# Where a Relu stands in ScalarE's queue: one edit for the inner layers, one for the first expert and one for the last weights of an attention and two-MoE kernel

## The chip, the cores and the metric

The kernel runs on one core of a Trainium2 chip. The metric is the device time of one execution in microseconds (us). The kernel before was run three times: 2096.52, 2099.13 and 2100.53 us, with a median of 2099.13 us. A separate profiled execution of it took 2101.21 us, and the trace of that execution covers a span of 2099.0 us.

The engines are named as the profile names them: PE is the matrix engine, PEld its weight load, DVE the vector engine, ACT the scalar engine, POOL the third elementwise engine, and SP the engine that issues nearly all DMAs. SPq is SP's DMA queue. The program lists the instructions of each engine in an order of their own, and the trace shows ACT, DVE and SP running theirs in that order.

## The reference

Three stages follow one another. `x` is 2304 tokens by 512 features between them.

```
# 1 attention: 4 x 8 heads, 1152 positions, 64 wide, queries averaged in pairs
attn = softmax(q.reshape(B, H, S//2, 2, D).mean(3) @ k.T / sqrt(D));  x = attn @ v
# 2 first MoE: P comes from exp(x @ w_gate) by 8 rounds of row and column scaling
for e in range(8): out += P[:, e:e+1] * (relu(x @ w1[e]) @ w2[e])     # w1[e] 512x1024, w2[e] 1024x512
# 3 second MoE: 8 experts with 4 slots each
slot_input = softmax_over_tokens(x @ phi).T @ x                       # 32 slots
slot_out[e] = relu(slot_input[e] @ w1[e]) @ w2[e]
out = softmax_over_slots(x @ phi) @ slot_out
```

## The kernel before, in words

**Numbers in two parts.** Matmuls of the first MoE work on fp32 values split in a high part and a low part: a CAST on ACT gives the high part, a subtraction on DVE the low part, and PE multiplies high by high, high by low and low by high. Such a split of a hidden activation is `h_split` (L731 to L735, tiles `ho`, three buffers); of a weight `p_split` or `f_hi` and `f_lo`; of `x` of block `i` `x0_split` (L589).

**Stages.** Attention ends near 505 us of the span. Then come experts 0 to 7 of the first MoE, one after another, over 9 blocks of 256 tokens, which are grouped in 3 units of 3 blocks. Expert 0 (506 to 699 us) has a plain first layer (`plain`, L786) and a second layer in a Strassen-Winograd form with 7 products (`product`, L805). Experts 1 to 6 (700 to 1775 us) have both layers in that form: 6 experts by 3 units are 18 units. Expert 7 (1775 to 2026 us) is plain and shares its time with the gate of the second MoE. The second MoE itself and the stores end the program.

**First layer of experts 1 to 6.** `chunk(e, u, n, f)` (L749) is one form `n` (0 to 6) for one quarter `f` (0 to 3) of the hidden features: 6 matmuls into a PSUM bank, then one elementwise step. For the last two forms, n = 5 and 6, the step has two instructions: DVE adds the bank to what lies in the hidden tile (L783), then ACT takes the Relu in place (L769, called at L784). The bank pool of these forms has two banks, so a chunk's matmuls need the add of two chunks earlier to be done.

**What orders the work.** The program builds a list of items, most of them one chunk, one plain quarter or one product. `at(k, f, late=...)` hangs other work behind item k. A loop (L1333) then calls each item and, behind it, what hangs there, in order of `late`. What an item itself issues therefore always stands ahead of what hangs behind it: in ACT's queue the Relu of chunk k stands ahead of an `h_split` CAST that hangs behind item k.

**Between the first experts.** `x0_split(0)` and `x0_store` prepare and store the split `x` of block 0; the split runs on DVE in the last part of attention. `prep` (L630) forms sums of `x` for the Strassen form of experts 1 to 6: four DVE sums, two CASTs on ACT and two subtractions, hung behind two items of each of blocks 1 to 4 and one of block 5. `fsum` (L507) forms sums of expert 1's weights on DVE, from staged quarters that SP loads (L474, L478) some items earlier; tuples `jobs` (L1284) and `FORMS0` (L1267) say behind which items. `base[b]` is the first item of block b, and a block has 11 items, p for a product of 12 matmuls and f for a plain quarter of 24, in the order "pfppfppfppf".

**Weights of the second MoE.** They are 32 MB, 64 units of 512 KB: 32 of w1, then 32 of w2. `load_m2(tags)` issues their DMAs on SP into tiles of earlier work that have come free, one name for each pool of buffers: `v`, `w` and `h` for weights and hidden tiles, `a`, `o`, `s` for `xa`, `ho` and `stg`. The tiles of `h` have 6 KB in each partition, and a load used 4 KB of them. The calls hang behind items of expert 7; 22 units are issued only when the first layer of the second MoE releases its w1 tiles (L1404). `layer2` (L1423) reads w2 in 8 steps of feature blocks f for each half dh of the output and each group G of four experts; `folded` (L1439) and `output` (L1453 to L1469) follow each half.

Of the kernel before, what the change touches and what calls it, by code (L numbers as in the profile page):

```python
# [405 lines left out]
def tile_attention__moe__softmoe(ctx, tc, q, k, v, w_gate, w1, w2, phi, m2_w1, m2_w2, out):  # L406
# [182 lines left out]
    def x0_split(i, copy=None):  # L589
        if i == 0:  # L590
            X0[i] = [x_tile("xs")[:, :512].rearrange("p (t z n) -> p t z n", t=2, z=2) for _ in range(4)]
            for kk in range(4):
                part = xa[i][:, kk].rearrange("p (t n) -> p t n", t=2)
                (copy or nc.scalar.copy)(X0[i][kk][:, :, 0], part)
                nc.vector.tensor_tensor(
                    out=X0[i][kk][:, :, 1], in0=part, in1=X0[i][kk][:, :, 0].bitcast(F32), op=ALU.subtract
                )
            return
        x = w_tile(("22", "11")[i % 2]).rearrange("p h (k t z n) -> p h k t z n", k=2, t=2, z=2)
        X0[i] = [x[:, kk // 2, kk % 2] for kk in range(4)]  # L600
        Xb[i] = x.rearrange("p h k t z n -> p h (k t z n)")
        for h in range(2):
            part = xa[i][:, 2 * h:2 * h + 2].rearrange("p k (t n) -> p k t n", t=2)
            nc.scalar.copy(x[:, h, :, :, 0], part)
            nc.vector.tensor_tensor(out=x[:, h, :, :, 1], in0=part, in1=x[:, h, :, :, 0].bitcast(F32), op=ALU.subtract)

    def x0_store(i):
        u = i // 3
        d = Xd[i] = dram_p.tile([128, 4, 512], F32, name=f"xd{i}")
        if i == 0:  # L610
            for kk in range(4):
                nc.sync.dma_start(out=d[:, kk], in_=X0[i][kk].rearrange("p t z n -> p (t z n)").bitcast(F32))
# [123 lines left out]

    seed, unit = {}, {}
    free = [2, 1, 3, 0]
# [10 lines left out]
    def chunk(e, u, n, f):  # L749
# [25 lines left out]
        if n == 1:  # L775
            relu(unit["A", 0][:, f], ps)
        elif n in (2, 3):
            nc.scalar.copy(unit["B", n - 2][:, f], ps)  # L778
        elif n == 4:
            relu(unit["A", 1][:, f], ps)  # L780
        else:
            o = unit["B", 6 - n][:, f]
            nc.vector.tensor_tensor(out=o, in0=ps, in1=o, op=ALU.add)  # L783
            relu(o, o)  # L784

# [188 lines left out]
    def tail2_steps(i):  # L974
# [3 lines left out]
        def tr(t):  # L978
            def f():
                if t == 0:  # L980
                    st["xT"] = stg_p.tile([128, 4, 256], F32, tag="stg", name="x2T")
                    if i == 0:
                        for _ in range(2):
                            HT.append(m_p.tile([128, 4, 256], F32, tag="ho", name="HT", bufs=3))
                            nc.gpsimd.memset(HT[-1], 0.0)  # L985
                        miscr = stg_p.tile([128, 1024], F32R, tag="stg", name="miscr")
                        T2["ct"] = [x_tile("ct") for _ in range(3)]
                        T2["c4"] = x_tile("c4", F32)
                        T2["o2"] = miscr[:, 768:1024]
                        misc = stg_p.tile([128, 1024], F32, tag="stg", name="misc")  # L990
# [115 lines left out]
    def slot_input():  # L1106
# [13 lines left out]
    w1t, w2t = {}, {}  # L1120
    queue = [("w1", e, z) for e in range(E) for z in range(2)] + [
        ("w2", dh, u) for dh in range(2) for u in range(8)
    ]

    def load_part(t, kind, a, b, lo, n):
        if kind == "w1":
            src = m2_w1[a][128 * lo:128 * (lo + n)].rearrange("(k p) f -> p k f", p=128)
            nc.sync.dma_start(out=t.rearrange("p (k f) -> p k f", k=n), in_=src)
            for x in range(n):
                w1t[a, lo + x] = t[:, 1024 * x:1024 * x + 1024]  # L1130
        else:
            f, e = 2 * (b % 4), 4 * (b // 4) + lo
            for c in range(2):
                src = m2_w2[e:e + n, 128 * (f + c):128 * (f + c) + 128, 256 * a:256 * a + 256].rearrange("e p d -> p e d")
                dst = t[:, 256 * n * c:256 * n * c + 256 * n]
                nc.sync.dma_start(out=dst.rearrange("p (e d) -> p e d", e=n), in_=src)
                for x in range(n):
                    w2t[a, e + x, f + c] = dst[:, 256 * x:256 * x + 256]

    rest = []  # L1140
    TAGS = {
        **{f"v{j}": (m_p, f"v{j}", 1) for j in range(7)},
        **{f"w{x}": (wp_p if x in EARLY else m_p, f"w{x}", 1) for x in ("11", "12", "S2", "S3", "22", "S1", "S4")},
        **{f"h{j}": (m_p, f"h{j}", 1) for j in range(4)},
        "a": (xa_p, "xa", NBLK), "o": (m_p, "ho", 3), "s": (stg_p, "stg", 4),
    }

    def load_m2(tags):
        for tag in tags.split():
            if not queue and not rest:  # L1150
                return
            pool, name, bufs = TAGS[tag]
            if tag[0] in "haos":
                kind, a, b = rest[0] if rest else queue.pop(0)
                n = 1 if kind == "w1" else 2
                lo = (2 * b if kind == "w1" else 0) + (n if rest else 0)
                rest[:] = [] if rest else [(kind, a, b)]
                t = pool.tile([128, 1536 if tag[0] == "h" else 1024], F32, tag=name, name="m2h", bufs=bufs)[:, :1024]
            else:
                kind, a, b = queue.pop(0)  # L1160
                n, lo = (2, 2 * b) if kind == "w1" else (4, 0)
                t = pool.tile([128, 2048], F32, tag=name, name="m2w", bufs=bufs)
            load_part(t, kind, a, b, lo, n)

# [80 lines left out]
    for n, (e, i, pos) in enumerate(blocks):  # L1245
# [21 lines left out]
    FORMS0 = (  # L1267
# [5 lines left out]
    for e in range(E - 1):  # L1273
        n = e + 1
        r = starts[e, 2] if e else base[8]
        if n < E - 1:
# [6 lines left out]
            else:  # L1283
                jobs = ((base[5] + 6, base[5] + 10, 2), (base[6] + 6, base[6] + 10, 2))  # L1284
            for (s, d, w), raws, names, stage in zip(jobs, (W1Q, Q), (WS, VS), (stage_w, stage_v)):
# [10 lines left out]

    where = [base[1 + n // 2] + (2, 7)[n % 2] for n in range(9)]
    for n, k in enumerate(where):
# [49 lines left out]
    for k in range(last + NBLK):  # L1348
# [18 lines left out]
        if q < 3 and j in (3, 6):  # L1367
            p_split(E - 1, q + 1 + j // 6 * 4, (("12", "S2", "S3"), ("v1", "v2", "v3"))[j // 6][q])
        load_m2({0: "v4", 1: "v5", 2: "v6", 7: "wS4", 9: "v0", 11: "w11", 18: "v1", 20: "w12", 26: "v2",
                 27: "wS2", 29: "a", 30: "a", 31: "a", 32: "a", 33: "a w22", 34: f"wS3 a wS1 h{order7[1]} o",  # L1370
                 35: f"a v3 h{order7[2]}"}.get(k, ""))
# [147 lines left out]
```

## Time and profile before

| what | value |
|---|---|
| three runs, median | 2096.52, 2099.13, 2100.53; 2099.13 us |
| profiled execution: its time, its span | 2101.21 us, 2099.0 us |
| PE busy | 2046.2 us, 97% of the span |
| DVE, ACT, POOL busy | 1426.4, 997.5, 410.4 us |
| chain of work that ended last, by engine | PE 80%, DVE 9%, ACT 4%, DMA 3% |
| DMA | 367.42 MB, mean 175 GB/s |

A row of the timeline gives start, duration, engine, line, operation, output <- inputs, shape and count; in brackets stands the idle time of that engine ahead of the row and what ended it. A row of the waits gives total us, number of waits, and the longest one. The clock column is the granted TensorE clock as a share of its full 2.4 GHz; 0.50 is the lower of its two levels, 1.2 GHz.

### The profile page before, as it was taken

The numbers are of one execution on the slowest core, as the hardware profiler recorded it, in microseconds if no ns is written. First come the engines' busy times: TensorE is split into PE (matmuls) and PEld (weight loads), VectorE is DVE, ScalarE is ACT, GpSimd is POOL, SyncE is SP. The second block draws the span as 40 slices with busy tenths as digits, with TensorE's granted clock in tenths as the row PEclk, the third lists the DMA queues.
The fourth block names the chain that finished last, engine by engine and source line by source line (L and its number), as shares of the span: only waits on it lengthen the run. The fifth ranks groups of instructions, "written<-read, shape, count | busy, mean of one in ns | idle before, by whom it ended". The sixth has DMA issues, their size and how long they took to land.

```text
span 2099.0 us, 38009 instructions
## 1 busy us (share of the span) xinstructions
PE 2046.2 (97%) x14800; PEld 1861.9 (89%) x14800; DVE 1426.4 (68%) x2601; ACT 997.5 (48%) x2110; POOL 410.4 (20%) x304
## 2 busy tenths in 40 slices
PE   7999999999999999999999999999999999999996
PEld 5777777777999999999999999999999999999863
DVE  5878778779676686776677677667767656544551
ACT  4666666666443644554454455445445444211231
POOL 6888888882000000000000000000000000000000
PEclk9999999999999999999999999999999999999997
DMA  7555565443457664456457345544744333577579
GB/s 187 139 134 125 119 148 136 114 114 126 166 182 258 214 223 151 153 186 209 139 183 249 133 161 192 190 165 151 262 141 159 113 111 113 201 267 254 211 244 278
DMA packets 198978, 367.42 MB, mean 175 GB/s; under 512 B 51472, under 2 KB 116304, under 8 KB 195792
## 3 DMA queue, kind: packets, MB, share of 16 engines
q1 hardware_dynamic: 196400, 363.53, 55.1%
q8 instruction: 117, 1.92, 0.4%
q10 hardware_dynamic: 2400, 1.47, 0.3%
q14 instruction: 61, 0.50, 0.1%
HBM read 276.38 MB, written 55.84 MB: 158 GB/s over the span
## 4 chain that ended last, share of the span: by engine, by line
PE 80%; DVE 9%; ACT 4%; DMA 3%; issue 2%; SPq 1%; POOL 0%; ACTq 0%; DVEq 0%; POOLq 0%
PE y L824 24%; PE seed L763 10%; PE g L763 9%; PE o L271 7%; PE se L245 7%; PE S L216 4%; DVE ht L728 2%; DVE hr L783 2%; PE g L859 2%; PE g L860 2%; PE g L858 2%; PE y L881 1%; PE y L882 1%; PE y L883 1%; ACT hr L769 1%
## 5 line engine op out<-in xcount | busy, mean ns | idle before, releaser
L824 PE MATMUL y<-v,ho 128*128 128x256 f32 x5292 | 691.9, 282 | 6.1 <-DVE ho L735 3.4
L824 PEld LDWEIGHTS y<-v,ho 128*128 128x128 f32 x5292 | 673.7, 190 | 11.6 <-issue 4.7
L763 PE MATMUL g<-xs,w 128*128 128x384 f32 x1728 | 337.2, 337 | 10.5 <-DVE hr L783 9.4
L256 POOL TENSOR_TENSOR acc<-acc,e 128x576 f32<-128x576 f32 x218 | 310.7, 1425 | 28.0 <-ACT e L248 14.1
L763 PEld LDWEIGHTS g<-xs,w 128*128 128x128 f32 x1728 | 292.3, 189 | 19.0 <-DVE hr L783 15.5
L217 DVE TENSOR_REDUCE m<-S 128x1 f32<-128x384 f32 x432 | 227.8, 554 | 76.3 <-PE S L216 60.6
L735 DVE TENSOR_TENSOR ho<-hr,ho 128x512 fp32r<-128x512 f32 x252 | 173.4, 688 | 144.4 <-ACT ho L734 143.8
L985 POOL MEMSET HT<- 128x1024 f32 x2 | 1.9, 958 | 1319.3 <-PE y L824 1319.3
L248 ACT ACTIVATE e<-se 128x288 f32<-128x288 f32 x576 | 213.3, 411 | 95.5 <-PE se L245 94.5
L836 DVE SCALAR_TENSOR_TENSOR acc<-y,P,acc 128x256 f32<-128x256 f32 x378 | 181.3, 480 | 106.7 <-PE y L824 105.2
L763 PE MATMUL seed<-xs,w 128*128 128x384 f32 x1296 | 247.6, 335 | 0.0
L763 PEld LDWEIGHTS seed<-xs,w 128*128 128x128 f32 x1296 | 220.2, 189 | 0.0
L735 DVE TENSOR_TENSOR ho<-ht,ho 128x512 fp32r<-128x512 f32 x189 | 129.6, 689 | 78.7 <-ACT ho L734 76.5
L734 ACT CAST ho<-hr 128x512 fp32r<-128x512 f32 x252 | 154.6, 615 | 45.1 <-PE y L824 31.8
L245 PE MATMUL se<-q,kd 128*128 128x288 f32 x576 | 166.6, 298 | 0.8 <-DVE kp L160 0.5
L769 ACT ACTIVATE hr<-hr 128x384 f32<-128x384 f32 x144 | 74.5, 525 | 195.3 <-DVE hr L783 195.3
L245 PE MATMUL se<-qm,kd 128*128 128x288 f32 x576 | 164.7, 295 | 0.0
L271 PE MATMUL o<-e,vr 128*64 128x288 f32 x1152 | 160.9, 414 | 0.0
L216 PE MATMUL S<-kd,q 128*128 128x384 f32 x384 | 143.3, 377 | 1.6 <-DVE m L217 1.4
L734 ACT CAST ho<-ht 128x512 fp32r<-128x512 f32 x189 | 115.7, 617 | 49.0 <-PE y L824 25.6
L778 ACT COPY hr<-seed 128x384 f32<-128x384 f32 x144 | 69.2, 480 | 127.9 <-PE seed L763 127.4
L271 PEld LDWEIGHTS o<-e,vr 128*64 128x64 f32 x1152 | 74.1, 136 | 50.4 <-issue 8.1
(211 smaller groups left out, 3036.3 us busy)
## 6 DMA issues: line engine op xcount, KB each, us to landing
stg<-in_moe_w_dram SPq DMA_DIRECT2D x96, 512.0 KB, 6.1
w<-xd SPq DMA_DIRECT2D x72, 512.0 KB, 4.7
xs<-xd0T SPq DMA_DIRECT2D x48, 384.0 KB, 3.9
xs<-xd1T SPq DMA_DIRECT2D x48, 384.0 KB, 4.9
xs<-xd2T SPq DMA_DIRECT2D x48, 384.0 KB, 3.6
kd<-kp SPq DMA_DIRECT2D x31, 576.0 KB, 5.9
xs<-xd0B SPq DMA_DIRECT2D x36, 384.0 KB, 3.6
xs<-xd1B SPq DMA_DIRECT2D x36, 384.0 KB, 3.9
```

The lines of the kernel that those rows point to most:

```text
L216: nc.tensor.matmul(ps, lhsT=w, rhs=r[:, 384 * n:384 * n + 384], start=True, stop=True)
L217: nc.vector.tensor_reduce(out=M_[ph][:, x, n:n + 1], in_=ps, axis=AX.X, op=ALU.max)
L245: nc.tensor.matmul(ps, lhsT=kd[:, z, 128 * c:128 * c + 128], rhs=y[:, h, g], start=z == 0, stop=z == 1)
L248: nc.scalar.activation(out=e[:, g], in_=ps, func=AF.Exp, scale=1.0 / 16)
L256: nc.gpsimd.tensor_tensor(out=acc_[ph], in0=acc_[ph], in1=e, op=ALU.add)
L271: nc.tensor.matmul(O_[ph][64 * g:64 * g + 64, :288], lhsT=raws["v"][pi][:, h, c, :], rhs=E_[ph, c][:, g], start=c == 0, stop=c == 8,)
L734: nc.scalar.copy(o[:, 0], p)
L735: nc.vector.tensor_tensor(out=o[:, 1], in0=p, in1=o[:, 0].bitcast(F32), op=ALU.subtract)
L763: nc.tensor.matmul(ps, lhsT=w[:, a, kk, 128 * f:128 * f + 128], rhs=x[:, :, b], start=first and kk + z == 0, stop=kk == 1 and z == 2, skip ...
L769: relu = lambda o, b: nc.scalar.activation(out=o, in_=b, func=AF.Relu)
L824: nc.tensor.matmul(ps, lhsT=o[:, x, c], rhs=v[:, w, c], start=first and c + z == 0, stop=c + z == 5, skip_group_check=not first,)
L836: nc.vector.scalar_tensor_tensor(out=y, in0=ps, scalar=p, in1=y, op0=ALU.mult, op1=ALU.add)
```

## The change

It has four parts.

**Relus of the last two forms.** `chunk` no longer issues the Relu of n = 5 and 6 at once, but puts it in a list `behind`. The loop over the items empties that list after all that hangs behind the item. Where nothing hangs there, ACT's order stays as it was; where an `h_split` hangs, its CAST now stands ahead of the Relu.

```diff
             nc.vector.tensor_tensor(out=o, in0=ps, in1=o, op=ALU.add)
-            relu(o, o)
+            behind.append(lambda: relu(o, o))
...
         for _, fs in sorted(after, key=lambda x: x[0]):
             for g in fs:
                 g()
+        while behind:
+            behind.pop(0)()
```

ACT, the last two forms of one unit of expert 2, before (`ho` and `hr` L734 are the splits, `hr` L769 the Relus):

```order
L734 CAST ho<-hr 128x512
L769 ACTIVATE hr<-hr 128x384
L734 CAST ho<-ht 128x512
L769 ACTIVATE hr<-hr 128x384 x2
L734 CAST ho<-ht 128x512
L769 ACTIVATE hr<-hr 128x384
L734 CAST ho<-hr 128x512
L734 CAST ho<-ht 128x512
L769 ACTIVATE hr<-hr 128x384 x2
L734 CAST ho<-hr 128x512
L769 ACTIVATE hr<-hr 128x384
L734 CAST ho<-hr 128x512
```

The same stretch after (lines are 6 higher):

```order
L740 CAST ho<-hr 128x512
L740 CAST ho<-ht 128x512
L775 ACTIVATE hr<-hr 128x384 x2
L740 CAST ho<-ht 128x512
L775 ACTIVATE hr<-hr 128x384
L740 CAST ho<-hr 128x512
L775 ACTIVATE hr<-hr 128x384
L740 CAST ho<-ht 128x512
L775 ACTIVATE hr<-hr 128x384 x2
L740 CAST ho<-hr 128x512 x2
L775 ACTIVATE hr<-hr 128x384
L740 CAST ho<-hr 128x512
```

Five of the eight Relus of a unit have moved behind the CAST that hung behind the same item. PE's order and DVE's order in these experts are as before.

**Block 0 of x.** `x0_split(0)` uses two tiles of the pool `stg` with two CASTs and two subtractions of 128x512, where it used four tiles of the pool `x` with four and four of 128x256; `x0_store` issues two DMAs in place of four.

**Expert 0's sums.** The nine `prep` sums and the sums of expert 1's weights hang behind other items, as do the loads of the latter.

```diff
-            jobs = ((base[5] + 6, base[5] + 10, 2), (base[6] + 6, base[6] + 10, 2))
+            jobs = ((base[5] + 6, base[6] + 2, 2), (base[6] + 10, base[7] + 3, 2))
-    where = [base[1 + n // 2] + (2, 7)[n % 2] for n in range(9)]
+    where = [base[b] + d for b, d in ((1, 4), (1, 8), (2, 4), (2, 8), (3, 2), (3, 5), (3, 9), (4, 2), (4, 9))]
```

In each tuple of `jobs` the first number is the item behind which the loads are issued, the second that of the first of four sums, the third the distance between them. In `FORMS0` form "11" goes from (-3, 2, 3) to (0, 6, 7) and "12" from (0, 8, 9) to (2, 8, 9).

DVE, around the first sum of weights in expert 0 (`stg` L507; `ho` are splits, `ht` sums of hidden tiles), before:

```order
L735 TENSOR_TENSOR ho<-hr,ho 128x512
L728 TENSOR_TENSOR ht<-hr 128x512
L728 TENSOR_TENSOR ht<-ht,hr 128x512
L507 TENSOR_TENSOR stg<-stg 128x1024
L735 TENSOR_TENSOR ho<-ht,ho 128x512 x2
L728 TENSOR_TENSOR hr<-hr 128x4x128
L728 TENSOR_TENSOR ht<-hr,ht 128x512
L507 TENSOR_TENSOR stg<-stg 128x1024
L836 SCALAR_TENSOR_TENSOR acc_8242<-y,acc_8242 128x256
L735 TENSOR_TENSOR ho<-hr,ho 128x512
```

After:

```order
L741 TENSOR_TENSOR ho<-hr,ho 128x512
L734 TENSOR_TENSOR ht<-hr 128x512
L734 TENSOR_TENSOR ht<-ht,hr 128x512
L741 TENSOR_TENSOR ho<-ht,ho 128x512 x2
L734 TENSOR_TENSOR hr<-hr 128x4x128
L734 TENSOR_TENSOR ht<-hr,ht 128x512
L842 SCALAR_TENSOR_TENSOR acc_8233<-y,acc_8233 128x256
L741 TENSOR_TENSOR ho<-hr,ho 128x512
L507 TENSOR_TENSOR stg<-stg 128x1024
```

The first weight sum has moved down past three splits, and where one stands in this stretch now, two stood before.

**Weights of the second MoE.** w2 is cut into pieces of 1 KB in each partition (one feature block of one expert and half), and `load_m2` fills each tile with as many pieces as it holds: 8, 6, 4, or 3 for a tile of the pool `x` (new tag). Two small tiles (`c4` and `o2`) move from the pools `x` and `stg` to `ht`, which frees two tiles `x` and one `stg`; a load into an `stg` tile is new behind item 28 of expert 7 (k = 28). The strings of tags change with it.

```diff
-                 27: "wS2", 29: "a", ..., 33: "a w22", 34: f"wS3 a wS1 h{order7[1]} o",
+                 27: "wS2", 28: "s", 29: "a", ..., 33: "a w22", 34: f"wS3 wS1 a h{order7[1]} h{order7[0]} o x x",
...
-    load_m2(f"a a h{order7[3]} h{order7[0]}")
+    load_m2(f"a a h{order7[3]}")
...
-                if kk % 2 and (e < 5 or 2 * e + kk // 2 == 13):
-                    load_m2("v4 v5 v6 wS4 v0 w11 v1 w12 v2 wS2 x x x w22".split()[2 * e + kk // 2])
+                if kk % 2 and 2 * e + kk // 2 < 10:
+                    load_m2("v4 v5 v6 wS4 v0 w11 v1 w12 v2 wS2".split()[2 * e + kk // 2])
```

SP's DMAs from the last load of `x` on (L1128 w1, L1136 w2), before:

```order
L676 DMA w<-xd_6544 128x1024 x2
L1128 DMA m2h<-in_moe_w_dram 128x1024 x2
L1128 DMA m2w<-in_moe_w_dram 128x2x1024 x2
L1128 DMA m2h<-in_moe_w_dram 128x1024
L1128 DMA m2w<-in_moe_w_dram 128x2x1024
L1136 DMA m2h<-in_moe_w_dram 128x2x256 x6
L1136 DMA m2w<-in_moe_w_dram 128x4x256 x2
L1136 DMA m2h<-in_moe_w_dram 128x2x256 x10
L1136 DMA m2w<-in_moe_w_dram 128x4x256 x22
```

After (L1148 w1, L1159 w2):

```order
L682 DMA w<-xd_6538 128x1024 x2
L1148 DMA m2h<-in_moe_w_dram 128x1024 x2
L1148 DMA m2w<-in_moe_w_dram 128x2x1024 x3
L1159 DMA m2h<-in_moe_w_dram 128x4x256 x2
L1159 DMA m2h<-in_moe_w_dram 128x2x256 x2
L1159 DMA m2h<-in_moe_w_dram 128x4x256 x2
L1159 DMA m2h<-in_moe_w_dram 128x3x256
L1159 DMA m2h<-in_moe_w_dram 128x256
L1159 DMA m2h<-in_moe_w_dram 128x2x256 x3
L1159 DMA m2w<-in_moe_w_dram 128x2x256
L1159 DMA m2w<-in_moe_w_dram 128x4x256
L1159 DMA m2w<-in_moe_w_dram 128x2x256
```

The bytes are the same. Of 64 units 46.5 now stand ahead of the first layer of the second MoE, where 42 did; the w2 DMAs are of 128 to 512 KB, where they were of 256 and 512 KB, and there are more of them.

## Rows read from the trace of the kernel before

**Rows 1.** Page, section 1: busy us (share of the span) and instructions of each engine.

```profile
PE 2046.2 (97%) x14800; PEld 1861.9 (89%) x14800; DVE 1426.4 (68%) x2601; ACT 997.5 (48%) x2110; POOL 410.4 (20%) x304
```

**Rows 2.** Table by stretch: PE, PEld, DVE, ACT, POOL busy; clock, DMA share, GB/s.

```profile
506.00:700.00 194.00, 187.91 (x1571) 181.72 (x1564) 136.30 (x282) 88.18 (x170) 0.00 (x0) 1.00 0.53 193
700.00:1775.00 1075.00, 1063.59 (x7472) 1054.69 (x7471) 747.54 (x1236) 526.04 (x963) 0.00 (x0) 1.00 0.52 172
2020.00:2044.00 24.00, 20.04 (x197) 10.95 (x199) 10.91 (x40) 7.35 (x29) 0.00 (x0) 0.93 0.96 310
2044.00:2070.00 26.00, 25.93 (x394) 15.19 (x390) 6.40 (x21) 7.58 (x23) 0.00 (x0) 1.00 1.09 349
2078.00:2099.00 21.00, 5.91 (x28) 4.42 (x20) 3.61 (x6) 3.68 (x7) 0.00 (x0) 0.50 0.69 172
```

**Rows 3.** Waits of the span: us in total, times, longest.

```profile
ACT ho L734 <- PE y L824: 57.4, 73, 1.5
...
PE g L763 <- DVE hr L783: 9.4, 19, 0.5
...
PE f L1430 <- DMA m2w<-in_moe_w_dram: 3.7, 5, 0.9
```

**Rows 4.** Timeline of one unit of expert 2, forms 5 and 6.

```profile
982.43 0.55 DVE L783 TENSOR_TENSOR hr<-g,hr 128x384 f32<-128x384 f32 x1
983.01 0.52 ACT L769 ACTIVATE hr<-hr 128x384 f32<-128x384 f32 x1 [1.54 <-DVE hr L783]
983.45 0.60 ACT L734 CAST ho<-ht 128x512 fp32r<-128x512 f32 x1
...
983.57 1.21 PE L763 MATMUL g<-xs,w 128*128 128x384 f32 x6
984.08 0.69 DVE L735 TENSOR_TENSOR ho<-ht,ho 128x512 fp32r<-128x512 f32 x1 [1.10 <-ACT ho L734]
984.69 0.55 DVE L783 TENSOR_TENSOR hr<-g,hr 128x384 f32<-128x384 f32 x1
...
985.30 1.33 PE L763 MATMUL g<-xs,w 128*128 128x384 f32 x6 [0.51 <-DVE hr L783]
```

**Rows 5.** Timeline of the end of attention: split of block 0.

```profile
482.15 1.50 DVE L594 CAST xs<-x 128x256 fp32r<-128x256 f32 x1
...
488.00 0.43 DVE L595 TENSOR_TENSOR xs<-x,xs 128x256 fp32r<-128x256 f32 x1
...
493.61 0.71 PE L282 MATMUL t<-acc,ones 128*64 128x288 f32 x4 [0.84 <-DVE acc L262]
```

**Rows 6.** Timeline of expert 0: the three longest waits of PE and what precedes them.

```profile
605.77 16.24 SPq L651 DMA_DIRECT2D xd2T<-xt  x5
...
617.00 0.62 ACT L648 CAST xt<-xs 128x512 fp32r<-128x512 f32 x1 [4.06 <-DVE xs L643]
...
618.98 1.70 PE L824 MATMUL y<-v,ho 128*128 128x256 f32 x12 [0.98 <-ACT acc L832]
...
628.28 2.01 SPq L474 DMA_DIRECT2D stg<-in_moe_w_dram  x4
...
635.78 1.22 DVE L507 TENSOR_TENSOR stg<-stg 128x1024 f32<-128x1024 f32 x1 [2.91 <-DMA stg<-in_moe_w_dram]
...
637.67 1.46 PE L824 MATMUL y<-v,ho 128*128 128x256 f32 x10 [1.92 <-DVE ho L735]
...
660.79 1.45 PE L824 MATMUL y<-v,ho 128*128 128x256 f32 x10 [0.94 <-DVE ho L735]
```

**Rows 7.** Timeline of the second MoE: its last loads and its end.

```profile
2038.03 32.21 SPq L1136 DMA_DIRECT2D m2w<-in_moe_w_dram  x22
...
2064.36 0.70 PE L1439 MATMUL fd<-misc,wg 128*128 128x256 f32 x2
...
2076.02 0.64 PE L1430 MATMUL f<-m2w,HT 128*32 128x256 f32 x8 [0.78 <-DMA m2w<-in_moe_w_dram]
2077.43 1.08 PE L1430 MATMUL f<-m2w,HT 128*32 128x256 f32 x8 [0.78 <-DMA m2w<-in_moe_w_dram]
...
2079.06 1.22 PE L1439 MATMUL fd<-misc,wg 128*128 128x256 f32 x2 [0.55 <-ACT misc L1435]
```

More of the change, by code (lines that the diff above doesn't have):

```diff
@@ L590, in x0_split @@
         if i == 0:
[L591 to L594, printed above, removed]
+            X0[i], Xb[i] = [], []
+            for h in range(2):
+                t = stg_p.tile([128, 1024], F32R, tag="stg", name="xt")
+                Xb[i].append(t)
+                x = t.rearrange("p (k t z n) -> p k t z n", k=2, t=2, z=2)
+                X0[i] += [x[:, 0], x[:, 1]]
+                part = xa[i][:, 2 * h:2 * h + 2].rearrange("p k (t n) -> p k t n", t=2)
+                (copy or nc.scalar.copy)(x[:, :, :, 0], part)
                 nc.vector.tensor_tensor(
-                    out=X0[i][kk][:, :, 1], in0=part, in1=X0[i][kk][:, :, 0].bitcast(F32), op=ALU.subtract
+                    out=x[:, :, :, 1], in0=part, in1=x[:, :, :, 0].bitcast(F32), op=ALU.subtract
                 )
@@ L610, in x0_store @@
         if i == 0:
-            for kk in range(4):
-                nc.sync.dma_start(out=d[:, kk], in_=X0[i][kk].rearrange("p t z n -> p (t z n)").bitcast(F32))
+            for h in range(2):
+                nc.sync.dma_start(
+                    out=d[:, 2 * h:2 * h + 2].rearrange("p k n -> p (k n)"), in_=Xb[i][h].bitcast(F32)
+                )
         else:
@@ L735, in h_split @@
         nc.vector.tensor_tensor(out=o[:, 1], in0=p, in1=o[:, 0].bitcast(F32), op=ALU.subtract)
-    seed, unit = {}, {}
+    seed, unit, behind = {}, {}, []
     free = [2, 1, 3, 0]
@@ L985, in f @@
                             nc.gpsimd.memset(HT[-1], 0.0)
-                        miscr = stg_p.tile([128, 1024], F32R, tag="stg", name="miscr")
                         T2["ct"] = [x_tile("ct") for _ in range(3)]
-                        T2["c4"] = x_tile("c4", F32)
-                        T2["o2"] = miscr[:, 768:1024]
+                        T2["c4"] = m_p.tile([128, 512], F32, tag="ht", name="c4", bufs=2)
+                        T2["o2"] = m_p.tile([128, 512], F32R, tag="ht", name="o2", bufs=2)[:, :256]
                         misc = stg_p.tile([128, 1024], F32, tag="stg", name="misc")
@@ L1120, in tile_attention__moe__softmoe @@
     w1t, w2t = {}, {}
[L1121 to L1138, printed above, removed]
+    queue = [("w1", e, 2 * z) for e in range(E) for z in range(2)]
+    pieces = [(dh, G, f, g) for dh in range(2) for G in range(2) for f in range(8) for g in range(4)]
     rest = []
     TAGS = {
[L1142 to L1145, printed above, removed]
+        **{f"v{j}": (m_p, f"v{j}", 1, 8) for j in range(7)},
+        **{f"w{x}": (wp_p if x in EARLY else m_p, f"w{x}", 1, 8) for x in ("11", "12", "S2", "S3", "22", "S1", "S4")},
+        **{f"h{j}": (m_p, f"h{j}", 1, 6) for j in range(4)},
+        "a": (xa_p, "xa", NBLK, 4), "o": (m_p, "ho", 3, 4), "s": (stg_p, "stg", 4, 4), "x": (wp_p, "x", 5, 3),
     }
@@ L1149, in load_m2 @@
         for tag in tags.split():
-            if not queue and not rest:
+            if not queue and not rest and not pieces:
                 return
[L1152 to L1163, printed above, removed]
+            pool, name, bufs, size = TAGS[tag]
+            t = pool.tile([128, 256 * size], F32, tag=name, name="m2w" if size == 8 else "m2h", bufs=bufs)
+            if queue or rest:
+                n = size // 4
+                e, k = rest.pop() if rest else queue.pop(0)[1:]
+                if n == 1 and k % 2 == 0:
+                    rest.append((e, k + 1))
+                src = m2_w1[e][128 * k:128 * (k + n)].rearrange("(k p) f -> p k f", p=128)
+                nc.sync.dma_start(out=t.rearrange("p (k f) -> p k f", k=n), in_=src)
+                for x in range(n):
+                    w1t[e, k + x] = t[:, 1024 * x:1024 * x + 1024]
+                continue
+            at_ = 0
+            while at_ < size and pieces:
+                dh, G, f, g = pieces[0]
+                n = min(4 - g, size - at_)
+                e = 4 * G + g
+                src = m2_w2[e:e + n, 128 * f:128 * f + 128, 256 * dh:256 * dh + 256].rearrange("e p d -> p e d")
+                dst = t[:, 256 * at_:256 * (at_ + n)]
+                nc.sync.dma_start(out=dst.rearrange("p (e d) -> p e d", e=n), in_=src)
+                for x in range(n):
+                    w2t[dh, e + x, f] = dst[:, 256 * x:256 * x + 256]
+                del pieces[:n]
+                at_ += n
     x0_store(0)
@@ L1369, in tile_attention__moe__softmoe @@
         load_m2({0: "v4", 1: "v5", 2: "v6", 7: "wS4", 9: "v0", 11: "w11", 18: "v1", 20: "w12", 26: "v2",
-                 27: "wS2", 29: "a", 30: "a", 31: "a", 32: "a", 33: "a w22", 34: f"wS3 a wS1 h{order7[1]} o",
+                 27: "wS2", 28: "s", 29: "a", 30: "a", 31: "a", 32: "a", 33: "a w22", 34: f"wS3 wS1 a h{order7[1]} h{order7[0]} o x x",
                  35: f"a v3 h{order7[2]}"}.get(k, ""))
@@ L1417, in tile_attention__moe__softmoe @@
     layer1(3)
-    assert not queue and not rest
+    assert not queue and not rest and not pieces
     o1, o2 = T2["l4"], T2["o2"]
```

2 rows, old and new, of the table FORMS0 are left out of this document.

## The prediction

> **What bounds the kernel now.** I read the page's busy times first: PE is busy 2046.2 of 2099.0 us [rows 1], so DVE, ACT and the DMAs matter only where PE waits for them, and all of PE's idle time is 52.8 us. No edit here takes a matmul away. So I looked for the waits of PE that the edits touch, by stretch. In expert 0 PE is idle 194.00 - 187.91 = 6.1 us, in experts 1 to 6 it is idle 1075.00 - 1063.59 = 11.4 us, and in the last 21.00 us it is busy for 5.91 [rows 2]. The list of waits names the causes [rows 3]: the first layer's matmuls wait 19 times, 9.4 us in all, for the add of the hidden tiles, and the second MoE's last matmuls wait 3.7 us for weights. The single waits of expert 0 and of the end of attention come from the timeline [rows 5, 6]. What follows takes them one by one.
>
> **Relus behind the CASTs (experts 1 to 6).** The wait in one unit reads like this [rows 4]. DVE's add ends at 982.43 + 0.55 = 982.98. ACT, idle for 1.54 us, then takes the Relu (983.01, 0.52), and only after it the CAST of `h_split` (983.45, 0.60), though what the CAST reads (`ht`) was ready before. DVE's next instruction is the subtraction that needs this CAST; it waits 1.10 us, runs from 984.08 for 0.69, and so the next add, whose bank PE is waiting for, starts at 984.69 and ends at 985.24. PE, done with the chunk before at 983.57 + 1.21 = 984.78, starts at 985.30, after 0.51 us. This adds up to one such wait per unit: 9.4 / 19 = 0.49 us, with 18 units.
>
> With the CAST ahead of the Relu, ACT does the CAST inside its 1.54 us of idle time (it needs 0.60), so it is done before 982.98. The subtraction then follows the add at once (982.98 to 983.67) and the next add waits for its matmuls only, which end where the following chunk starts, near 983.57; it runs 983.67 to 984.22, and the bank is free 984.78 - 984.22 = 0.56 us before PE asks for it. The Relu itself follows the CAST or the add, whichever is later; the next readers of the tile are the `ht` sums, several chunks on. So 18 x 0.51 = 9.2 us go. The bounds are 0 (the CAST is late for another reason, and the same subtraction stays late) and 9.4, the whole row [rows 3]; loss below 0 is a rival below. I take 9.2, since the cover of 0.56 us is as large as the wait. What is late next is nothing on PE in this stretch up to that slack; of the 11.4 us of idle time 2.2 remain, which no edit touches.
>
> **Block 0 of x in two halves.** DVE spends 482.15 to 488.43 on the eight instructions [rows 5], the first three at 1.5 us each, later ones at 0.43 or less. Four instructions of twice the size move the same elements. If the first three still take 1.5 and the last 0.69 (a subtraction of 128x512, rows 4), the list ends near 487.4, 1.0 us earlier. PE's wait at 493.61 for DVE's sum (`acc` L262), which comes later in DVE's order, is 0.84 us; I take all of it, 0.8, with bounds of 0 (DVE waits for something else in between) and 1.0. Two stores fewer on SP I cost at nothing: no wait of PE in these rows is for a store of block 0.
>
> **Expert 0's sums.** Three waits of PE, 0.98 + 1.92 + 0.94 = 3.84 us [rows 6]. In the first, ACT stands at a CAST of `prep` that waits 4.06 us for DVE's sums; behind it in ACT's queue is the copy of `y` whose bank PE wants. This is the last of the nine; it goes from item 2 of block 5 to item 9 of block 4, four items earlier, and away from the loads and sums of the weights. In the second, DVE stands at the first weight sum, waiting 2.91 us for the load; the subtraction behind it, 0.69 us, is what PE wants (635.78 + 1.22 + 0.69 = 637.69, against PE's 637.67). The load is late because SP issued it at 628.28: SP stood from 605.77 for 16.24 us at stores of `prep`. Both change: the `prep` stores come earlier in the program, and the sum follows its load by 7 items in place of 4, some 15 us where a block of 11 items takes about 23. For the third the distance stays 4 items, but the queue ahead of that load is shorter too, since the first four sums and their stores end earlier. I take all three, 3.8 us. The bounds: 5.4 if the stretch's smaller waits go too, out of 6.1 us idle [rows 2]; on the other side a moved sum can hold up another split, at worst the third wait stays and two like the second come in new places: 0.98 + 1.92 - 2 x 1.92 = -0.9.
>
> **The second MoE's weights.** From 2038.03 the stream is SP's queue alone: 22 units of 512 KB take 32.21 us, 1.46 us each [rows 7]. PE's last groups of eight matmuls wait for one unit each, and the end follows the last landing. Ahead of that the engines of the DMA move 310 GB/s in 2020 to 2044 and 349 in 2044 to 2070 [rows 2]: (349 - 310) / 349 x 24.00 = 2.7 us of transfer lie idle in the first. The edit loads one unit earlier into an `stg` tile, at a time when the queue has room, which takes 1.46 us out of the full stretch, and offers 46.5 units in place of 42 ahead of layer 1, so that the queue does not stand at a release in 2020 to 2044. The last landing comes up to 1.46 + 2.7 = 4.2 us earlier. PE's waits for weights are 3.7 us, so they go, and the matmuls become the limit. With them goes the fall of the clock: in 2078 to 2099 the granted clock is 0.50, and the last group took 1.08 us where its equal just before took 0.64, the product behind it 1.22 where the same one took 0.70 in the first half [rows 7]. That is 0.44 + 0.52 = 0.96. In all 3.7 + 1.0 = 4.7 us. The bounds are 2 (one unit earlier, 1.46, and half of the clock's 0.96) and 6 (the output matmuls go quicker too). The tail behind the last product (copies and stores) keeps its length.
>
> The pieces cost more DMAs of 128 to 512 KB in place of 256 and 512 KB. In the trace the mix with 256 KB DMAs (2020 to 2044, 310 GB/s) and the 512 KB DMAs alone (2044 to 2070, 349) differ by 11%, and the first stretch has other reasons for it; I cost it at nothing, with the rival below. The Trainium skill, "DMA: Bandwidth & Descriptors", section Bandwidth, asks for DMAs of at least 1 MiB, and measures 64 KB at 0.95 us and 1 MB at 6.15 us (341 GB/s), issued from GpSimd. An estimate on the line between the two is 2.0 us for 256 KB, 131 GB/s, and by it the change would end near 2110 us, slower. The trace disagrees where it can be read: 512 KB DMAs in a full queue reach 349 GB/s [rows 2], above that page's figure for 1 MB, so the size of one DMA does not set the pace of a queue with others behind it.
>
> **The sum.** 9.2 + 0.8 + 3.8 + 4.7 = 18.5 us. The profiled execution took 2101.21 us, its span 2099.0 and 2.2 us around it; that is 2.1 above the median of the runs, 2099.13. So 2101.2 - 18.5 = 2082.7 for a profiled execution, and 2099.1 - 18.5 = 2080.6 for the median. I predict 2081 us, with its own range of 2076 to 2086: all upper bounds together give 9.4 + 1.0 + 5.4 + 6 = 21.8, which is 2077.3, and 1.5 us less than that for the scatter of the runs.
>
> **The rivals.**
> - *Expert 0 gives nothing.* The moved sums hit other splits, as its lower bound has it. For it speaks that a split still stands right behind a sum in DVE's order; against it, that the loads are issued earlier. 2080.6 + 3.8 to 4.7 = about 2085.
> - *The stall at the Relu moves instead of going.* The subtraction is early, but another instruction on DVE or the `ho` buffer of the CAST is late by as much in half of the units. Only half of 9.2 comes: 2085; with none, 2090. For it speaks that ACT waits 73 times, 57.4 us, for products to free an `ho` buffer [rows 3].
> - *The pieces slow the stream.* If w2 moves at the 310 GB/s of the stretch with smaller DMAs and not at 349, the 11.9 MB of 2044 to 2078 (34 x 349) take 38.3 us in place of 34, 4.3 more; with 1.46 for the unit loaded earlier the last landing is 2.8 us later than before, and the 4.7 do not come: 2080.6 + 4.7 + 2.8 = 2088. For it speaks the difference of the two rates, against it that the first stretch also holds waits for tiles to come free. (The page above would have it dearer.)
> - *The CAST blocks the Relu (slower).* The CAST, now at ACT's head, waits for its `ho` buffer, 57.4 / 73 = 0.79 us in the mean [rows 3]; the Relu behind it is late, the `ht` sums behind the Relu on DVE are late, and the next product with them. If one such wait a unit reaches PE, 18 x 0.79 = 14.2 us come and the 9.2 don't go: 2099.1 - 9.3 + 14.2 = 2104. It decides from 9.3 / 18 = 0.52 us a unit on. Against it: in the unit's rows the CAST waits for nothing once the Relu is out of the way, so its buffer was free by 983.45 at the latest, and the 57.4 us lie in all of the second layers, not in these two forms.
> - *Nothing of it shows.* The waits of PE are replaced one by one by others: 2095 to 2103.
>
> **Chances.** The forecast 0.62; expert 0 nothing 0.12; the Relu part half or none 0.10; a slower stream 0.07; slower 0.04; no change 0.05. A measurement of this kernel tells about 0.2% from no change, 4.2 us. All but the last two lie over 4.2 us below 2099.1: faster 0.91, same 0.05, slower 0.04. The range of 2075 to 2091 holds the forecast and the rivals on the faster side, but for the scatter at its ends.
>
> **What would show it.** Right: in forms 5 and 6 ACT's CAST starts ahead of the add's end, DVE's subtraction follows the add without a gap, and PE's 19 waits for the add are gone from the list. In expert 0 the three waits are gone, and SP issues the first weight loads before 625. At the end, no wait of PE for weights in the last groups, and a clock of 1.00 up to the last product. Wrong: the same total of PE's waits for the add under another name, a row of PE or DVE waiting on ACT's Relu, waits for weights at new places of layer 2, or the last landing no earlier.

## The result, and the profile after

The changed kernel takes 2067.87 us (median of four runs, 2067.37 to 2069.30) against 2098.83 for the kernel before: a ratio of 0.9854, 95% interval 0.9837 to 0.9871. That is 31.0 us less, where 18.5 were forecast; 2067.87 lies below the range of 2075 to 2091. The direction was right, and three of the four places gave something; the size was not right.

The page of the changed kernel, section 1 and the first line of the chain in section 4, which answer to [rows 1]:

```profile
PE 2035.3 (98%) x14800; PEld 1860.8 (90%) x14800; DVE 1431.2 (69%) x2597; ACT 1007.7 (49%) x2110; POOL 411.8 (20%) x304
...
PE 92%; DVE 2%; DMA 2%; ACT 1%; SPq 1%; issue 0%; ACTq 0%; DVEq 0%
```

PE issues the same 14800 matmuls, yet its busy time fell by 10.9 us. Hold on to that: a change of order takes no work away, so busy time before held something else. Two things turn out to be in it: matmuls that ran at the lower clock, and pieces of PE's waits.

The table by stretch, against [rows 2] (the last three stretches begin some 25 us earlier, since the program does):

```profile
506.00:700.00 194.00, 191.86 (x1595) 186.32 (x1595) 141.85 (x290) 92.09 (x178) 0.00 (x0) 1.00 0.54 194
700.00:1775.00 1075.00, 1074.23 (x7626) 1073.10 (x7626) 765.51 (x1259) 539.39 (x967) 0.00 (x0) 1.00 0.52 174
1995.00:2019.00 24.00, 20.04 (x186) 10.63 (x184) 11.18 (x40) 7.29 (x28) 0.00 (x0) 0.86 1.06 347
2019.00:2040.00 21.00, 21.00 (x342) 11.95 (x338) 3.20 (x15) 4.99 (x18) 0.00 (x0) 1.00 1.10 348
2051.00:2067.50 16.50, 2.77 (x18) 2.32 (x18) 3.42 (x6) 3.00 (x6) 0.00 (x0) 0.67 0.81 215
```

By this table PE is idle in experts 1 to 6 for 0.77 us, where it was 11.4. The weight stream ran at 310 GB/s in the stretch ahead of layer 1 and now runs at 347.

The unit of [rows 4] in the changed kernel (L775 is the Relu, L740 and L741 the split, L789 the add; "..." marks rows left out, here and below):

```profile
966.94 2.25 PE L769 MATMUL g<-xs,w 128*128 128x384 f32 x12
967.13 0.60 ACT L740 CAST ho<-ht 128x512 fp32r<-128x512 f32 x1
...
968.18 0.56 DVE L789 TENSOR_TENSOR hr<-g,hr 128x384 f32<-128x384 f32 x1
968.66 0.68 DVE L741 TENSOR_TENSOR ho<-ht,ho 128x512 fp32r<-128x512 f32 x1
968.78 0.53 ACT L775 ACTIVATE hr<-hr 128x384 f32<-128x384 f32 x1 [1.04 <-DVE hr L789]
...
969.26 0.55 DVE L789 TENSOR_TENSOR hr<-g,hr 128x384 f32<-128x384 f32 x1
...
970.45 2.25 PE L769 MATMUL g<-xs,w 128*128 128x384 f32 x12
```

The CAST starts 1.05 us ahead of the add, the subtraction follows the add without a gap, and the second add ends at 969.81. PE runs the two chunks as one group of 12 from 970.45: the second, which waited before, goes without a break.

Both kernels have the same matmuls in the same order, so the start of the n-th matmul can be compared in the two traces. By how much the changed one is earlier, in us from each span's start, at points of the trace before:

```
100 us: 1.6   478: 1.9   506: 2.4   699: 8.1   1800: 24.8   2054: 23.8   last matmul: 30.7
so: attention up to 478 us 1.9, its end 0.5, expert 0 5.7, experts 1 to 6 16.7,
    begin of the second MoE -0.9, its end 6.9
```

The -0.9 goes with the clock: the stretch at the lower clock that both traces have at the begin of the second MoE makes the mean 0.86 in this trace and 0.93 in the one before [rows 2]. From trace to trace it differs, and the trace of part 4 alone has none there.

### The profile page after: what moved, and what is told of

The parts are those of the page before. It is cut to its first block, busy times and chain, and to the rows that moved or that the text cites. A ratio compares the mean times of both kernels' runs of the same rounds, so it can differ in the third digit from the quotient of the medians.

```text
span 2067.5 us, 37998 instructions
## 1 busy us (share of the span) xinstructions
PE 2035.3 (98%) x14800; PEld 1860.8 (90%) x14800; DVE 1431.2 (69%) x2597; ACT 1007.7 (49%) x2110; POOL 411.8 (20%) x304
## 3 DMA queue, kind: packets, MB, share of 16 engines
q8 instruction: 117, 1.92, 0.4%
## 4 chain that ended last, share of the span: by engine, by line
PE 92%; DVE 2%; DMA 2%; ACT 1%; SPq 1%; issue 0%; ACTq 0%; DVEq 0%
PE y L830 30%; PE g L769 14%; PE seed L769 10%; PE o L271 7%; PE se L245 7%; PE S L216 5%; PE g L865 2%; PE g L866 2%; PE g L864 2%; PE y L887 1%; PE g L800 1%; PE y L888 1%; PE y L889 1%; PE g L802 1%; PE g L801 1%; PE f L1401 1%
## 5 line engine op out<-in xcount | busy, mean ns | idle before, releaser
L769 PE MATMUL g<-xs,w 128*128 128x384 f32 x1728 | 330.6, 335 | 1.0 <-ACT seed L777 0.8
L769 PEld LDWEIGHTS g<-xs,w 128*128 128x128 f32 x1728 | 293.9, 189 | 1.8 <-ACT seed L777 1.1
L769 PE MATMUL seed<-xs,w 128*128 128x384 f32 x1296 | 247.8, 335 | 0.0
L741 DVE TENSOR_TENSOR ho<-hr,ho 128x512 fp32r<-128x512 f32 x252 | 172.9, 686 | 79.0 <-ACT ho L740 78.3
L769 PEld LDWEIGHTS seed<-xs,w 128*128 128x128 f32 x1296 | 220.2, 189 | 0.2 <-DMA xs<-xd0T 0.2
L740 ACT CAST ho<-hr 128x512 fp32r<-128x512 f32 x252 | 155.7, 619 | 68.2 <-PE y L830 61.2
L741 DVE TENSOR_TENSOR ho<-ht,ho 128x512 fp32r<-128x512 f32 x189 | 129.5, 689 | 55.4 <-ACT ho L740 55.3
L740 ACT CAST ho<-ht 128x512 fp32r<-128x512 f32 x189 | 116.3, 619 | 52.4 <-PE y L830 30.2
L775 ACT ACTIVATE hr<-hr 128x384 f32<-128x384 f32 x144 | 75.8, 526 | 106.2 <-DVE hr L789 105.7
```

Source lines behind the costliest of these rows:

```text
L740: nc.scalar.copy(o[:, 0], p)
L741: nc.vector.tensor_tensor(out=o[:, 1], in0=p, in1=o[:, 0].bitcast(F32), op=ALU.subtract)
L769: nc.tensor.matmul(ps, lhsT=w[:, a, kk, 128 * f:128 * f + 128], rhs=x[:, :, b], start=first and kk + z == 0, stop=kk == 1 and z == 2, skip ...
L775: relu = lambda o, b: nc.scalar.activation(out=o, in_=b, func=AF.Relu)
```

## The experiments

**Part 1 alone, and the rest without it.**

```diff
 relu_only: the kernel before with
+            behind.append(lambda: relu(o, o))      # cut: and the loop over behind, as in the change
 no_relu: the changed kernel with
+            relu(o, o)
```

> The kernel before with the first part of the change alone (Relus of forms 5 and 6 behind the CASTs). Both theories: PE's 19 waits for the add of the hidden tile, 9.4 us in the list of waits, are gone. Theory A (a wait costs PE more than the idle time of its row, since the matmul ahead of it is recorded for 0.33 us though the next one could have started 0.17 us after it, and the gap behind the wait is 0.1 us longer; some 0.8 to 0.9 us a unit): 16 us less than before, near 2082.5. Theory B (a wait costs its idle time, 0.5 us a unit, as I predicted, and the rest of the surplus comes from an interplay with the other parts): 9 us less, near 2089.5.

> The changed kernel with the first part alone undone. Theory A: 16 us more than the changed kernel, near 2084, and 18 or 19 waits for the add are back. Theory B: 9 us more, near 2077.

Measured: 2081.69 us against 2098.63, ratio 0.9921 (0.9907 to 0.9934), 16.9 us less; and 2085.23, 17.4 us more than the changed kernel. Theory A's time is met and theory B's 9 us is not: by its interval this part alone is worth 13.8 to 19.5 us, and it is worth as much in company. In the list of waits of the second kernel the wait is back, with the same 9.4 us as in [rows 3]:

```profile
PE g L769 <- DVE hr L789: 9.4, 19, 0.5
```

So this part takes away 9.4 us of idle time in that row, and 17 us of run time.

**A wait of a size that can be set.** In the changed kernel, reductions of the identity matrix with an unused result are put on DVE ahead of the add that holds the bank of chunk (5, 3), in each of the 18 units.

```diff
             o = unit["B", 6 - n][:, f]
+            if (n, f) == (6, 1):
+                for _ in range(3):           # delay3; 8 in delay8, 12 in delay12
+                    nc.vector.tensor_reduce(out=junk, in_=ident, axis=AX.X, op=ALU.max)
             nc.vector.tensor_tensor(out=o, in0=ps, in1=o, op=ALU.add)
```

> The changed kernel with three small reductions on DVE (about 0.25 us each, their result unused) put ahead of the add of chunk (6, 1) in each of the 18 units, which holds the bank that chunk (5, 3) needs. In the changed kernel that add ends 1.7 us ahead of the matmul that needs the bank. Cover theory: 0.7 us fit in, the time stays within 1 us of the changed kernel. Rival (the slack is needed elsewhere, for the splits behind): 18 waits, 5 us or more.

> The same with eight reductions, about 2 us: the add ends some 0.3 us after PE could have started. Theory A: each of the 18 waits costs the idle time of its row plus about 0.3 us: with rows of about 0.15 us, 18 x 0.45 = 8 us more than the changed kernel. Theory B: the time lost equals the idle time that the list of waits shows, 3 to 5 us.

> The same with twelve reductions, about 3 us. Theory A: idle time of the rows (about 1.1 us each, 20 us in all) plus 18 x 0.3 = 5 us. Theory B: the idle time alone. The two runs together tell a fixed surplus per wait from one that grows with the wait.

Measured: 2068.84, 2086.41 and 2111.22 us. Three reductions (0.92 us in one unit of the trace) are covered: 1.0 us over the changed kernel, which the scatter doesn't tell from nothing, and no such wait in the list. With eight, and then with twelve, the list of waits shows:

```profile
PE g L770 <- DVE hr L793: 12.0, 18, 1.1
```

```profile
PE g L770 <- DVE hr L793: 35.1, 18, 2.4
```

The waits came out longer than I had sized them for eight (0.67 us each, not 0.15): eight reductions take 2.53 us in the trace and not 2. What matters is the comparison with the time. Against the covered run, 2068.84, eight cost 17.6 us for 12.0 us idle and twelve 42.4 us for 35.1: a surplus of 5.6 and 7.3 us over 18 waits, 0.31 and 0.41 each. The surplus is a price per wait and does not grow in proportion: by proportion the second would have cost 35.1 x 17.6 / 12.0 = 51 us. Matmul by matmul the trace with eight loses 16.9 us against the changed kernel in experts 1 to 6, and 12.0 + 18 x 0.27 is 16.9. The trace with twelve loses 41.7; of these some 1.5 us are not in the waits but in matmuls behind the first of them, where the granted clock is 0.50 from 737.6 to 740.8.

One wait by the timeline: with eight, the unhindered chunk and under it the waiting one; then, with twelve, a waiting one:

```profile
974.62 1.21 PE L770 MATMUL g<-xs,w 128*128 128x384 f32 x6
...
976.47 1.31 PE L770 MATMUL g<-xs,w 128*128 128x384 f32 x6 [0.64 <-DVE hr L793]
```

```profile
983.51 1.31 PE L770 MATMUL g<-xs,w 128*128 128x384 f32 x6 [1.92 <-DVE hr L793]
```

Here is where the surplus sits. Six matmuls take 1.21 us and twelve take 2.25 (rows of the changed kernel above), so each further one takes (2.25 - 1.21) / 6 = 0.173 us, and 1.21 - 6 x 0.173 = 0.17 us at the end of a group are the last matmul's record running on past the moment at which the next one would have started. An idle time in brackets begins only behind that record: it is 0.17 short. And the group behind a wait takes 1.31 in place of 1.21, since its second matmul starts 0.28 and not 0.17 us after the first. So a wait costs its bracket plus 0.17 + 0.10 = 0.27 us, at 0.64 us and at 1.92 us alike. Start to start, the gap ahead of the waiting matmul is 0.98 and 2.26 us in the two kernels and 0.85 in the kernel before (bracket 0.51), against 0.17 unhindered: each is its bracket and twice 0.17, one of them the normal distance and one the piece that the bracket leaves out.

**Part 3 alone, and the rest without it.**

```diff
 exp0_only: the kernel before with, no_exp0: the changed kernel without
+            jobs = ((base[5] + 6, base[6] + 2, 2), (base[6] + 10, base[7] + 3, 2))
+    where = [base[b] + d for b, d in ((1, 4), (1, 8), (2, 4), (2, 8), (3, 2), (3, 5), (3, 9), (4, 2), (4, 9))]
+        ("11", 0, 6, 7), ("12", 2, 8, 9), ...
```

> The kernel before with expert 0's sums and loads respaced, and nothing else. Theory A (three waits of 3.84 us idle are worth 4.6, with 0.6 for a wait of 0.46 that goes too, 1.3 for the gate's wait at 524 and 1.3 lost to two new waits): about 5.5 us less than before, near 2093. Theory B (idle time of the rows): 3.8 less, near 2095. If the moved sums help only together with block 0's tiles: less than 2 us.

> The changed kernel with the third part alone undone (expert 0's sums where they were). If the parts add: 6.5 us more than the changed kernel, near 2074.4. If block 0's tiles, taken from the pool of the staged sums, cost something only where the sums are not respaced (alone that part lost time in expert 0): 8 to 10 more, near 2077.

Measured: 2092.11 us, ratio 0.9967 (0.9955 to 0.9980), 6.5 us less; and 2076.47, 8.6 us more than the changed kernel. What PE waits for in expert 0 with the part alone, the whole list of 506 to 700 us:

```profile
PE g L763 <- ACT seed L771: 0.8, 1, 0.8
PE y L824 <- DVE v L535: 0.6, 1, 0.6
```

The three waits of [rows 6] are gone, and with them one of 0.5 and the gate's wait of 1.0 us. Start to start, with the slower second matmul, the three cost 1.25, 2.18 and 1.20 us in the trace before: 0.26 or 0.27 us more than each bracket, as in the first layer. The other two cost 0.6 and 1.3.

**Part 2 alone, and the rest without it.**

```diff
 x0_only: the kernel before with, no_x0: the changed kernel without
+            for h in range(2):                 # cut: the lines for block 0
+                t = stg_p.tile([128, 1024], F32R, tag="stg", name="xt")
```

> The kernel before with block 0 of x split in two halves, and nothing else. Theory A (the 2.5 us that the changed kernel's trace is ahead in its first 100 us are scatter of one execution, since no edit touches that stretch): 0.5 to 0.8 us less than before, near 2098.2. Rival (the tiles moved from one pool to another also change something at the start): 2 to 3 us less, near 2096.

> The changed kernel with the second part alone undone (block 0 of x in four tiles again). If the parts simply add, as measured alone (16.9, 6.5 and 6.5 us gained, 1.7 lost by this one): 2068.8 less the interplay, so equal to the changed kernel within 1.5 us, or up to 1.7 faster. If the 2.6 us by which the whole gains more than its parts come from this part's working with the respaced sums: about 2070.5, slower by 2 to 3.

Measured: 2100.64 us, ratio 1.0007 (0.9998 to 1.0016); and 2068.25, 0.4 us from the changed kernel. The part is worth nothing that can be measured. In the split the larger instructions took longer while POOL was adding, by the timeline of the changed kernel, to be read beside [rows 5]:

```profile
480.31 1.64 DVE L598 CAST xt<-x 128x512 fp32r<-128x512 f32 x1
481.98 1.78 DVE L599 TENSOR_TENSOR xt<-x,xt 128x512 fp32r<-128x512 f32 x1
...
483.68 1.65 DVE L598 CAST xt<-x 128x512 fp32r<-128x512 f32 x1
485.36 0.69 DVE L599 TENSOR_TENSOR xt<-x,xt 128x512 fp32r<-128x512 f32 x1
```

They take 5.74 us from first start to last end, where the eight took 6.28: 0.5 less and not 1.0. In both kernels three of these instructions fall into POOL's adds, and a larger one took little longer there than a smaller one. Side by side with the trace before, the matmuls of part 2 alone gain 0.5 us from 478 to 506 us, and 0.7 is given back by 535 us, at a second-layer weight that DVE splits later. Its trace is also 2.5 us ahead of the trace before in the first 100 us, with no shorter time. All eleven traces of the experiments are 1.5 to 3.5 us ahead at 478 us: the 1.9 us up to there belong to the one profiled execution of the kernel before, not to the change.

One thing in this trace is not the part's work. The second product of [rows 6], whose ten matmuls take 1.46 us there, reads:

```profile
635.28 2.51 PE L830 MATMUL y<-v,ho 128*128 128x256 f32 x10 [1.97 <-DVE ho L741]
```

Behind this wait the granted clock is 0.50 from 635.4 to 638.6, and some 1.5 us are lost; the trace of part 4 alone has the same from 636.7 to 639.9, behind a wait of 2.04. The changed kernel without part 3 keeps 1.00 there behind a wait of 2.07, as does the kernel before behind its 1.92, so executions differ. The kernels with part 3 have no such wait in expert 0.

**Part 4 alone, and its new load later.**

```diff
 tail_only: the kernel before with load_m2, its strings and the two small tiles of the change
 s_later: the changed kernel with
-                 27: "wS2", 28: "s", 29: "a", 30: "a", 31: "a", 32: "a", ...
+                 27: "wS2", 29: "a", 30: "a", 31: "a", 32: "a s", ...
```

> The kernel before with the fourth part alone (w2 in 1 KB pieces, the small tiles moved, one load earlier). Theory A (as the matmuls of the two traces stand side by side): 6 us less than before, near 2093. Theory B (the predicted 4.7): near 2094. If the gain at the end is due to another state of the queue, left by the other parts: within 2 us of before.

> The changed kernel with the new load into a staging tile behind item 32 of expert 7 in place of item 28. Theory of the prediction (one unit taken out of the full stretch of the weight stream is worth 1.46 us, at 28 and still at 32 if the queue has room there): the same as the changed kernel within 1 us. If the queue is already full from item 32 on: up to 1.5 us slower, and waits of PE for weights are back.

Measured: 2092.11 us, ratio 0.9968 (0.9956 to 0.9981), 6.5 us less; and 2070.09 (2068.86 to 2070.97) with the load later, 2.2 us over the changed kernel at ratios to the kernel before that overlap (0.9849 to 0.9881 and 0.9837 to 0.9871). The later load brings no wait of PE for weights back, and its matmuls stand within 1 us of the changed kernel's up to the end; I take it as no change. That one unit more ahead of the full stretch decides was not shown: there is room to spare without it.

The end of the changed kernel, to be read beside [rows 7] and the rows of the kernel before under it:

```profile
2040.57 0.70 PE L1441 MATMUL fd<-misc,wg 128*128 128x256 f32 x2
...
2045.84 3.66 PE L1432 MATMUL f<-m2w,HT 128*32 128x256 f32 x64
2050.05 0.70 PE L1441 MATMUL fd<-misc,wg 128*128 128x256 f32 x2 [0.55 <-ACT misc L1437]
2052.22 2.84 PE L1455 MATMUL op<-o,ct 128*128 128x256 f32 x18 [1.46 <-DVE o L1445]
```

```profile
2071.58 0.64 PE L1430 MATMUL f<-m2w,HT 128*32 128x256 f32 x8 [0.42 <-DMA m2w<-in_moe_w_dram]
2073.09 0.64 PE L1430 MATMUL f<-m2w,HT 128*32 128x256 f32 x8 [0.87 <-DMA m2w<-in_moe_w_dram]
2074.59 0.64 PE L1430 MATMUL f<-m2w,HT 128*32 128x256 f32 x8 [0.86 <-DMA m2w<-in_moe_w_dram]
...
2081.74 4.18 PE L1453 MATMUL op<-miscr,ct 128*128 128x256 f32 x18 [1.47 <-DVE miscr L1443]
```

The last groups of eight run as one group of 64 without a wait for weights, the product takes 0.70 and not 1.22, and the output matmuls 2.84 us, where they took 4.18 before. The table by stretch for these output matmuls, changed kernel and kernel before, has a granted clock of 1.00 and then of 0.50:

```profile
2052.20:2055.10 2.90, 2.77 (x18) 2.31 (x18) 2.13 (x4) 1.66 (x3) 0.00 (x0) 1.00 0.86 261
```

```profile
2081.70:2085.95 4.25, 4.18 (x18) 3.92 (x18) 2.49 (x4) 2.35 (x4) 0.00 (x0) 0.50 0.28 72
```

## Why the prediction was wrong in size

| step | forecast, us | alone, us | undone, us | what was wrong |
|---|---|---|---|---|
| 1 Relus | 9.2 | 16.9 | 17.4 | price of a wait |
| 2 block 0 | 0.8 | -1.7 (no change) | 0.4 | mechanism: given back |
| 3 expert 0 | 3.8 | 6.5 | 8.6 | price, and the gate's wait |
| 4 weights | 4.7 | 6.5 | not run | price, and the output matmuls |
| all | 18.5 | 28.2 as a sum | | 31.0 measured |

**The failed step** is the price of a wait. "This adds up to one such wait per unit: 9.4 / 19 = 0.49 us" took the idle time in the list of waits for the time that the wait costs. A wait for the add cost 0.78 us in place of 0.51: its bracket, the 0.17 that the bracket leaves out, and the 0.10 at the second matmul. The delays show the same 0.27 at other lengths of the wait, and so do the three waits of expert 0. The Trainium skill, "Perfetto Trace Analysis", section Tensor Engine Instruction, states that the end of a matmul in a profile is computed from its size and not observed. The trace agrees, with a record that runs 0.17 us past the next possible start; what it does to idle time that page does not say, and the runs show it.

By the runs part 1 gives a surplus of 0.39 to 0.42 per wait, and the traces say where the rest is. Of the 16.7 us that experts 1 to 6 gain, the 19 waits make 14.5. A wait of a product for its split (0.45 us idle, at 760.30 in the trace before) went too and makes 0.7. And the pair of chunks ahead of the waiting one takes 2.30 us in the kernel before and 2.25 in the changed one:

```profile
980.00 2.30 PE L763 MATMUL g<-xs,w 128*128 128x384 f32 x12
982.14 1.60 PE L824 MATMUL y<-v,ho 128*128 128x256 f32 x12
```

Its eighth matmul starts 0.03 us late and its twelfth 0.01, which no row of the waits shows. Differences of this kind, below 0.04 us each, make 1.3 us.

The fall of PE's busy time by 10.9 us is the other face of it. The 19 + 3 waits, at 0.27, had 5.9 us booked as work, and the lower clock at the end made 0.44 + 0.52 + 1.34 = 2.3 us of longer records.

Beyond the price three terms were left out: the gate's wait and the one of 0.5 in expert 0, 1.9 us start to start; the output matmuls, 1.34 us; and the small pieces above. Against them part 2's 0.8 did not come. Counted from 478 us on, the matmuls of the two traces differ by 28.9 us, and the interval of the ratio goes from 27.1 to 34.2 us, so what is left to the 31.0 is within the scatter.

**Point by point.** *Relus*: the mechanism was right in each step; CAST ahead of the add, subtraction at the add's end, 19 waits gone. The slack behind it is larger than the 0.56 us that I gave it. The prediction let the second add wait for matmuls that end near 983.57; they end near 982.3, as a product (the row at 982.14 above) stands between. In the changed kernel that add ends at 969.81 and its bank is wanted at 970.45 + 6 x 0.173 = 971.49, 1.68 us later, and 0.92 us of reductions went in for nothing. *Expert 0*: the three waits went for the reasons given. SP issues the loads of the first sums at 621.07, 7.2 us before the 628.28 of [rows 6], in a trace that is 2.8 us ahead there, and no sum waits for a load. Three waits at 3.84 + 3 x 0.27 make 4.65; I had left out the one of 0.5 and the gate's wait of 1.0, which the respaced sums take away too. I held 5.4 for the upper bound, and the 6.5 measured lie above it. *Block 0*: wrong, as above. PE's wait for `acc` fell from 0.8 to 0.3 us, and the later split of a weight took that back; its bound of 0 holds. *Weights*: the waits for weights went, and the clock falls only behind the output matmuls. The five waits cost 0.61 + 1.05 + 1.05 + 0.97 + 0.96 = 4.64 us start to start and not 3.7, some 0.19 more each; the output matmuls, at a granted clock of 1.00 in place of 0.50, gave 4.18 - 2.84 = 1.34 us, which I had counted only in the bound of 6.

**The rivals.** *The pieces slow the stream*: fell. With DMAs of 128 to 512 KB the stretch ahead of layer 1 went from 310 to 347 GB/s. Its lower rate before came from tiles not yet free; What SP's queue waited for most among the engines in that stretch, before (2020 to 2044 us) and after (1995 to 2019), fell from 9.9 to 1.0 us:

```profile
SPq L1136 <- PE sl L1080: 9.9, 3, 5.1
```

```profile
SPq L1159 <- PE slT L1114: 1.0, 1, 1.0
```

The Trainium skill, "DMA: Bandwidth & Descriptors", section Bandwidth, asks for DMAs of at least 1 MiB. The trace disagrees for a queue kept full: 347 GB/s in this stretch. The 2110 us that the prediction took from that page, without the steps from 131 GB/s to it, did not come. *The CAST blocks the Relu*: its sign is there and its price is not. ACT now waits 144 times, 91.3 us in all, for products to free an `ho` buffer, where [rows 3] have 73 and 57.4:

```profile
ACT ho L740 <- PE y L830: 91.3, 144, 1.3
```

But the list of PE's waits has none for a Relu, and none for the add. *Expert 0 gives nothing*: fell, by itself and in company.

**What adds up and what doesn't.** The parts alone sum to 28.2 us. Part 3 is worth 8.6 in company and 6.5 alone; part 2 costs 1.7 or nothing alone and nothing in company. It would fit both that part 2's tiles disturb the sums at their old places, but the traces do not show it: without part 3 the changed kernel has the same two waits of PE for a split in expert 0 as the kernel before (2.9 us), and what part 2 gives back, 0.7 alone, 1.1 without part 3 and 0.9 in the changed kernel, lies ahead of 520 us each time, before the sums. What the trace of part 2 alone loses beyond that in expert 0 are the 1.5 us at the lower clock. With intervals of some 3 us on each, how much of the 2.8 is the clock in some executions and how much is scatter stays open.

## What to carry to other kernels

Price a wait of PE from start to start: the gap ahead of the waiting matmul less the normal one, and the slower second matmul behind it. Idle time in a list of waits leaves out a piece that does not grow with the wait (0.27 us in the first layer here, 0.19 at the last weights), so count the waits first and their length second: many short ones are worth far more than their sum. Where one instruction on an elementwise engine holds up a queue that the next bank depends on, look for an instruction ahead of it whose readers are far away: here a Relu that nobody needed soon stood ahead of a CAST that everybody behind did.

## What the runs showed of the hardware beyond this

While POOL was adding, DVE instructions of twice the size took little longer: 1.64 to 1.78 us for 128x512 against 1.50 to 1.52 for 128x256; once POOL was done, the subtractions took 0.69 against 0.43. So the merging was worth little because POOL's adds covered three instructions in both kernels, three of eight before and three of four after. A queue of weight loads kept 347 to 349 GB/s with 256 KB DMAs mixed in and with 512 KB ones alone. The granted clock can fall behind a single wait of PE: to 0.50 for some 3 us behind waits of 1.97, 2.04 and 2.37 us, in three of the traces, and not behind one of 2.07 in another.
